# Attention stage of a fused kernel: PSUM banks split by use, the turning of outputs one step later, and row sums of squares taken after the biases

## The chip, the core and the metric

The kernel runs on one NeuronCore of one Trainium2 chip. The metric is the device time of one execution in microseconds (us). Five engines run their own instruction streams in order and wait for each other through semaphores: TensorE (PE), VectorE (DVE), ScalarE (ACT), GpSimd (POOL) and SyncE (SP, which here issues all transfers).

## The reference

```
def phi(x):
    proj = np.einsum('bhsd,md->bhsm', x, omega)
    sq = np.sum(x * x, axis=-1, keepdims=True) / 2.0
    h = proj - sq
    h = h - np.max(h, axis=-1, keepdims=True)
    return np.exp(h) / np.sqrt(m)
q_p, k_p = (phi(q_s), phi(k_s))
kv = np.einsum('bhsm,bhsd->bhmd', k_p, v)
z = np.sum(k_p, axis=2)
num = np.einsum('bhsm,bhmd->bhsd', q_p, kv)
den = np.einsum('bhsm,bhm->bhs', q_p, z)[..., None] + 1e-06
return (num / den).astype(np.float32)
```

This linear attention (batch 4, 8 heads, 576 positions, 64 wide, 128 features, all fp32) is followed by two feed-forward stages on the 2304 tokens: one gated by SiLU, and one of 8 experts that are all computed and mixed by weights. Those two are most of the time and are not touched by the change.

## The kernel before

**Stages.** The attention comes first and is a software pipeline written by hand. Its inputs are cut into 36 chunks of 128 partitions x 512 elements (8 groups of 64). Chunk 0 and chunk 17 are k tails (the last 64 positions of all heads), 18 and 35 are q tails; of the others the odd ones are k and the even ones q. A step of the pipeline does one piece of work for each of several chunks: `ORDER` (line 64) is a list of pairs of a piece and its lag, and in step s a piece with lag n is done for chunk s - n. The list is walked once per step, and each engine executes its instructions in the order in which the walk emits them. So `ORDER` sets the order on every engine.

**The pieces**, by line:
- `s0` (L481 to L484, POOL): squares a chunk of the next step and adds them pairwise, 64 to 16. `s0r` (L491, L492, DVE) adds up the rest and puts the sum of squares into `tri`.
- `s2p` (L510, PE): 16 matmuls project a chunk into two PSUM banks. `s2m` (L514, DVE, twice) takes the maxima from the banks; `s2b` and `s2c` (L518, L522, DVE) make the bias `bi` of them and of the sum of squares; `s2x` (L529, ACT, 8 instructions) takes the exponentials from the two banks.
- `s3`: for k, 40 matmuls with v (L550, PE) into a bank `kv`; for q, 8 transposes (L554, PE) into two banks. `s3a` (ACT) copies them to SBUF: L563 for k, L567 twice for q.
- `s4` (L580, PE): 32 matmuls of a q chunk with `kv` into two banks; `s4d`, `s4r`, `s4n` (L592, L597, L602, DVE) divide by the denominator.
- `s5` (L612, PE): 4 transposes turn the output of a q chunk into one bank; `s5a` (L623, ACT) copies it to `xh`, `s5b` (L628, DVE) writes the rest, bank less `xh`, to `xl`.
- `pump`: two slots in a step, each of which does one item of background work, the conversion of the next stage's weights. A task of 10 items has DVE items L198, L200, L202, L205, L207, ACT items L196 and L180 (the latter in the slot of L202), and POOL items L211, L214, L182; the other slots are empty. Six tasks are queued for the attention, from step 3 on.

In an even step PE thus projects a k chunk and does L580 and L554 for q chunks; in an odd step it projects a q chunk and does L550 for a k chunk. A pair of steps handles one k and one q chunk.

**Banks.** The eight PSUM banks are handed out in rings (`RINGS`): each use takes the next bank of its ring, and uses whose rings are equal share one turn.

**Buffers.** `xx`, the squares, lies in the fourth quarter of the tile `at0`, and the chunks themselves turn in the other three.

**End.** From step NCH + 1 = 37 on, each step also calls `next(m1)`, which emits 12 matmuls of the first feed-forward stage (L700 to L702), and the rings change to `DRAIN`.

Of the kernel before, what the change touches and what calls it, by code (L numbers as in the profile page):

```python
# [11 lines left out]
F32 = mybir.dt.float32  # L12
F32R = mybir.dt.float32r
# [7 lines left out]
P = 128  # L21
B, H, S, D = 4, 8, 576, 64
# [29 lines left out]
class Kernel:  # L52
    def __init__(self, tc, x, v, vt, omega, wg, wv, wo, w2g, w1, w2, out):
# [7 lines left out]

    ORDER = [("s3a0", 3), ("s0r", 0), ("s5a", 7), ("s2p", 1), ("s2m0", 1), ("s40", 4), ("s41", 4),
# [3 lines left out]
    RINGS = dict(tr3=(0, 3), tr5=(4, 5, 6, 7, 2, 1), pr=(4, 5, 6, 7, 2, 1), nu=(4, 5, 6,  # L68
                 7, 2, 1), a=(0, 1, 2, 3), b=(4, 5, 6, 7))

    DRAIN = dict(RINGS, tr3=(4, 5), tr5=(4, 5), nu=(6, 7))


    EARLY = 1
# [287 lines left out]
    def run(self):  # L362
        tc, nc = self.tc, self.nc
        with ExitStack() as ctx:
            self.cst = ctx.enter_context(tc.tile_pool(name="cst", bufs=1))
            self.raw = ctx.enter_context(tc.tile_pool(name="raw", bufs=1))
            self.ar1 = self.cst.tile([P, 6144], F32R, name="ar1")
            self.ar2 = self.cst.tile([P, 4096], F32R, name="ar2")
            self.af = ctx.enter_context(tc.tile_pool(name="af", bufs=1))
            psum = ctx.enter_context(tc.tile_pool(name="psum", bufs=1, space=PSUM))  # L370
            self.banks = [psum.tile([P, 512], F32, tag=f"b{i}", name=f"bank{i}") for i in range(4)]
            upper = ExitStack()
            psum = upper.enter_context(tc.tile_pool(name="upper", bufs=1, space=PSUM))
            self.banks += [psum.tile([P, 512], F32, tag=f"b{i}", name=f"bank{i}") for i in range(4, 8)]
            self.turns, self.rings, self.nquad = {}, self.RINGS, 0
            ident = self.cst.tile([P, P], F32, name="ident")
            make_identity(nc, ident)
            self.ident = ident
            self.xh = self.cst.tile([P, KC, NTOK], F32R, name="xh")
            self.xl = self.cst.tile([P, KC, NTOK], F32R, name="xl")  # L380
            self.cv = self.af.tile([P, 1024], I32, tag="cv", name="cv")
            park = ctx.enter_context(tc.tile_pool(name="park", bufs=1, space=bass.MemoryType.DRAM))
            self.park = park.tile([P, NB, KC, NBK], F32, name="parked")
            self.w1f = park.tile([P, NG2, 14, 512], F32, name="w1forms")
            self.w2f = park.tile([P, NG2, 7, 2, 2, 256], F32, name="w2forms")
            self.pd = park.tile([(NT - 6) * E, P], F32, name="pweights")
            with tc.manual_schedule():
                m1 = self.moe1()
                self.attention(m1)
                for _ in m1:  # L390
                    pass
                rest = self.moe2()
                upper.close()
                psum = ctx.enter_context(tc.tile_pool(name="pairs", bufs=1, space=PSUM))
                self.pairs = [psum.tile([P, 1024], F32, tag=f"b{i}", name=f"pair{i}") for i in range(2)]
                self.thirds(*rest)
# [3 lines left out]
    def attention(self, m1):  # L400
        tc, nc = self.tc, self.nc
        if True:
            af, ident = self.af, self.ident
            t0 = af.tile([P, 4, 512], F32, tag="t0", name="at0")
# [10 lines left out]
            def turn(name, n):  # L415
                rot[name] = (rot.get(name, -1) + 1) % n
                return rot[name]
# [8 lines left out]
            w = 8 * ZW  # L426
            vzts = [t4[:, NVZ + i] for i in range(2)] + [bx[:, 2048 + i * w:2048 + (i + 1) * w].rearrange(
                "p (a d) -> p a d", d=ZW) for i in range(2)]
            xts = [bx[:, i * 512:(i + 1) * 512] for i in range(4)]

            chunks = [("k", 0, None, None)]
# [8 lines left out]
            NCH = len(chunks)  # L440
# [5 lines left out]
            def load(i):  # L446
                side, bp, hp, j = chunks[i]
                c = st[i]
                n = 8 if hp is None else 2 * hp + j
                k = turn("x", 3)  # L450
                xt = xts[turn("xt", 4)]
                c["xt"] = xt.rearrange("p (a t) -> p a t", t=P)
                c["x"] = t0[:, k].rearrange("p (a d) -> p a d", d=D)
                for w, t in ((1, xt), (0, t0[:, k])):
                    nc.sync.dma_start(t, self.x["qk".index(side), w, bp, n])
                c["idx"] = (lambda a, h: 2 * a + h) if hp is None else (lambda a, h: 4 * h + a)

            def loadv(i):
                side, bp, hp, j = chunks[i]
                c = st[i]  # L460
                if side == "q":
                    return
                if hp is None:
                    c["vz"] = vzts[2 * bp:2 * bp + 2]
                    for j in range(2):
                        nc.sync.dma_start(c["vz"][j].rearrange("p a d -> p (a d)"), self.vt[bp, j])
                else:
                    z = c["vz"] = vz[nvz[0] % NVZ]
                    nvz[0] += 1
                    nc.sync.dma_start(z.rearrange("p a d -> p (a d)"), self.v[bp, 2 * hp + j])  # L470

            def s0(i):
                c = st[i]
                sqv = c["x"]
                if i < self.EARLY:
                    c["xx"] = t2[:, i].rearrange("p (a d) -> p a d", d=D)
                    c["tri"] = sm.tile([P, 8, 3], F32, tag="tri", name=f"tri{i}", bufs=4)
                    nc.scalar.activation(c["xx"], sqv, AF.Square)
                    return
                xx = t0[:, 3].rearrange("p (a d) -> p a d", d=D)  # L480
                nc.gpsimd.tensor_tensor(xx, sqv, sqv, op=ALU.mult)  # L481
                c["tri"] = sm.tile([P, 8, 3], F32, tag="tri", name=f"tri{i}", bufs=4)
                nc.gpsimd.tensor_tensor(xx[:, :, 0:32], xx[:, :, 0:32], xx[:, :, 32:64], op=ALU.add)
                nc.gpsimd.tensor_tensor(xx[:, :, 0:16], xx[:, :, 0:16], xx[:, :, 16:32], op=ALU.add)  # L484
                c["xx"] = xx
# [144 lines left out]

            pump = lambda i: self.attn_pump()
            fns = dict(s0=s0, s0r=s0r, s2=s2, s2p=s2p, s2b=s2b, s2c=s2c, s4r=s4r, s5=s5, s5a=s5a, s5b=s5b, pump=pump)
            halves = dict(s2m=s2m, s2x=s2x, s3=s3, s3a=s3a, s4=s4, s4d=s4d, s4n=s4n)

            def stage(n):
                if n in fns:
                    return fns[n]
                g, h = halves[n[:-1]], int(n[-1])
                return lambda i: g(i, h)

            order = [(stage(n), k) for n, k in self.ORDER]
            nc.sync.dma_start(om, self.omega)
            nc.vector.tensor_scalar(om, om, SCALE, None, op0=ALU.mult)
            load(0)
            load(1)
            s0(0)
            for step in range(NCH + 7):
                if step == NCH + 1:
                    self.rings = self.DRAIN
                if step + 2 < NCH:  # L650
                    load(step + 2)
                if step == 0:
                    loadv(0)
                if step + 1 < NCH:
                    loadv(step + 1)
                for fn, n in order:
                    i = step - n
                    if 0 <= i < NCH:
                        fn(i)
                self.attn_hook(step)  # L660
                if step >= NCH + 1:
                    next(m1)

    def attn_hook(self, step):
# [10 lines left out]
    def moe1(self):  # L675
# [43 lines left out]
        def ounit(g, b, us):  # L719
# [29 lines left out]
            if g == NG1 - 1 and b >= 2:  # L749
# [3 lines left out]
                else:  # L753
                    src = t4[:, 3:7, :] if b == 4 else tt[b][:, 0:4, :]
                    nc.sync.dma_start(self.park[:, b], src)

        self.side = self.sums()
        self.m1_open = True
        pend = None
# [779 lines left out]
```

## Time and profile before

| | us |
|---|---|
| median of 3 runs | 2054.8 (2054.72 to 2054.96) |
| profiled execution | 2054.87 |
| its span, first to last instruction | 2053.1 |
| PE busy in the span | 2016.2 (98%) |
| DVE, ACT, POOL busy | 1363.7, 805.5, 1035.1 |
| attention: first of 12 matmuls of the next stage starts at | 141.31 |
| exponentials of chunk 0, 9, 35 start at | 11.10, 41.36, 138.61 |

The span is 1.77 us shorter than the profiled execution. The attention takes the first 7% of it. A row of the timeline merges instructions of one line that follow each other on an engine; "x8" is their count, and in brackets stand the idle time of the engine before them and what ended it.

### The profile page before, as it was taken

The page shows a single profiled execution, that of the slowest core. Times are in us where ns is not written, and L with a number is a line of the kernel's source. Part 1 is how long each engine was busy: PE and PEld are TensorE (multiplying, and loading weights), DVE is VectorE, ACT ScalarE, POOL GpSimd, SP SyncE. Part 2 cuts the span into 40 slices and gives each one's busy share as a digit, 9 for nine tenths or more (in the row PEclk, how much of TensorE's full clock was granted, in tenths as well). Part 3 has the DMA queues.
Part 4 walks back from the last instruction along what each step waited for, and adds up shares of the span by engine and source line. Part 5 has one row for each costly group of instructions (what it writes and reads, how often), then busy time and mean ns, then how long its engine had stood idle before and what let it go on. Part 6 is the DMA issues. An engine that isn't in the chain of part 4 may idle for free.

```text
span 2053.1 us, 34001 instructions
## 1 busy us (share of the span) xinstructions
PE 2016.2 (98%) x12556; PEld 1948.0 (95%) x12556; DVE 1363.7 (66%) x2320; ACT 805.5 (39%) x1805; POOL 1035.1 (50%) x1019
## 2 busy tenths in 40 slices
PE   7899999999999999999999999999999999999998
PEld 6789999999998899899898999999999999999998
DVE  6876788778657654454455666666778766666666
ACT  7874433333345344344343433333233433232322
POOL 6755666656425455554752443434454544444443
PEclk9999999999999999999999999999999999999999
DMA  7635555556226657667668888888878887788784
GB/s 245 218 120 164 162 188 182 178 164 190 76 99 241 241 203 275 233 242 281 226 248 295 259 264 260 258 263 286 272 248 277 289 258 261 263 257 261 246 267 153
DMA packets 238133, 467.84 MB, mean 228 GB/s; under 512 B 20272, under 2 KB 110096, under 8 KB 233872
## 3 DMA queue, kind: packets, MB, share of 16 engines
q1 hardware_dynamic: 237968, 465.68, 68.1%
q8 instruction: 99, 1.62, 0.3%
q14 instruction: 66, 0.54, 0.1%
HBM read 340.25 MB, written 125.35 MB: 227 GB/s over the span
## 4 chain that ended last, share of the span: by engine, by line
PE 91%; DVE 5%; POOL 2%; issue 1%; ACT 1%; DMA 0%; SPq 0%; DVEq 0%; POOLq 0%; ACTq 0%
PE bank L1061 12%; PE bank L1309 7%; PE bank L1311 7%; PE bank L1310 7%; PE pair L1401 7%; PE pair L1403 7%; PE pair L1402 7%; PE bank L700 5%; PE bank L701 5%; PE bank L702 5%; PE bank L1002 4%; PE bank L1004 4%; PE bank L1003 4%; PE bank L732 2%; PE bank L733 2%; PE bank L734 2%
## 5 line engine op out<-in xcount | busy, mean ns | idle before, releaser
L1413 DVE TENSOR_TENSOR sums<-pair,sums 128x768 f32<-128x768 f32 x209 | 198.6, 951 | 43.6 <-PE pair L1403 43.6
L1309 PE MATMUL bank<-xh,ar 128*128 128x384 f32 x564 | 188.5, 334 | 0.9 <-DVE last L1347 0.9
L1311 PE MATMUL bank<-xh,ar 128*128 128x384 f32 x564 | 188.4, 334 | 0.0
L1310 PE MATMUL bank<-xl,ar 128*128 128x384 f32 x564 | 188.4, 334 | 0.0
L1077 DVE SCALAR_TENSOR_TENSOR ac<-bank,mt,ac 128x512 f32<-128x512 f32 x84 | 63.1, 751 | 130.7 <-PE bank L1061 130.7
L1401 PE MATMUL pair<-xh,ar 128*128 128x384 f32 x344 | 115.0, 334 | 0.2 <-DVE sums L1413 0.2
L1403 PE MATMUL pair<-xh,ar 128*128 128x384 f32 x344 | 114.9, 334 | 0.0
L1402 PE MATMUL pair<-xl,ar 128*128 128x384 f32 x344 | 114.9, 334 | 0.0
L1309 PEld LDWEIGHTS bank<-xh,ar 128*128 128x128 f32 x564 | 105.9, 188 | 1.3 <-DVE last L1347 1.2
L1311 PEld LDWEIGHTS bank<-xh,ar 128*128 128x128 f32 x564 | 105.9, 188 | 0.0
L1310 PEld LDWEIGHTS bank<-xl,ar 128*128 128x128 f32 x564 | 105.9, 188 | 0.0
L714 ACT CAST ar<-mt 128x384 fp32r<-128x384 f32 x72 | 37.0, 514 | 169.0 <-DVE mt L711 169.0
L700 PE MATMUL bank<-xh,ar 128*128 128x384 f32 x288 | 96.7, 336 | 0.1
L702 PE MATMUL bank<-xh,ar 128*128 128x384 f32 x288 | 96.2, 334 | 0.0
L702 PE MATMUL bank<-xh,ar1b 128*128 128x384 f32 x288 | 96.2, 334 | 0.0
L701 PE MATMUL bank<-xl,ar 128*128 128x384 f32 x288 | 96.2, 334 | 0.0
L700 PE MATMUL bank<-xh,ar1b 128*128 128x384 f32 x288 | 96.2, 334 | 0.0
L701 PE MATMUL bank<-xl,ar1b 128*128 128x384 f32 x288 | 96.2, 334 | 0.0
L1002 PE MATMUL bank<-xh,ar 128*128 128x384 f32 x264 | 89.2, 338 | 0.9 <-DVE mt L1036 0.6
L1004 PE MATMUL bank<-xh,ar 128*128 128x384 f32 x264 | 88.6, 336 | 0.1
L529 ACT ACTIVATE at<-bank,bi 128x128 f32<-128x128 f32 x288 | 78.4, 383 | 26.0 <-DVE bi L522 18.8
L1003 PE MATMUL bank<-xl,ar 128*128 128x384 f32 x264 | 88.3, 335 | 0.0
(370 smaller groups left out, 6637.6 us busy)
## 6 DMA issues: line engine op xcount, KB each, us to landing
ar<-w2forms SPq DMA_DIRECT2D x144, 512.0 KB, 4.4
ar<-w1forms SPq DMA_DIRECT2D x141, 512.0 KB, 4.8
ar1b<-w1forms SPq DMA_DIRECT2D x62, 512.0 KB, 4.8
ar1b<-w2forms SPq DMA_DIRECT2D x61, 512.0 KB, 4.4
w2forms<-ar SPq DMA_DIRECT2D x224, 128.0 KB, 4.0
w1forms<-ar SPq DMA_DIRECT2D x22, 1280.0 KB, 6.9
sumsraw<-in_w_dram SPq DMA_DIRECT2D x32, 512.0 KB, 4.4
w2forms<-sumsraw SPq DMA_DIRECT2D x128, 128.0 KB, 2.7
```

What stands on the lines that cost most here:

```text
L700: nc.tensor.matmul(t, hi[:, c, fs], self.xh[:, c, cs], start=(c == 0), stop=False)
L701: nc.tensor.matmul(t, hi[:, c, fs], self.xl[:, c, cs], start=False, stop=False)
L702: nc.tensor.matmul(t, lo[:, c, fs], self.xh[:, c, cs], start=False, stop=(c == KC - 1))
L1002: nc.tensor.matmul(g, ah[:, c, :], bh[:, c, :], start=(first and c == 0), stop=False, skip_group_check=not first)
L1061: nc.tensor.matmul(y, a, w[:, fi % 2, ds], start=(first and x == 0 and k == 0 and fi == fis[0]), stop=(last and x == 1 and fi == fis[-1]))
L1309: nc.tensor.matmul(g, w[:, 0, d], bh[:, d, :], start=bool(first and d == 0), stop=False, skip_group_check=not first)
L1310: nc.tensor.matmul(g, w[:, 0, d], bl[:, d, :], start=False, stop=False, skip_group_check=not first)
L1311: nc.tensor.matmul(g, w[:, 1, d], bh[:, d, :], start=False, stop=(d == 1), skip_group_check=not first)
L1401: nc.tensor.matmul(y, w[:, k, 0, ds], h, start=(k == 0), stop=False)
L1402: nc.tensor.matmul(y, w[:, k, 0, ds], l, start=False, stop=False)
L1403: nc.tensor.matmul(y, w[:, k, 1, ds], h, start=False, stop=(k == 1))
L1413: v.tensor_tensor(a[n], pair, a[n], op=ALU.add)
```

## The change

It rewrites `ORDER` and `RINGS`, gives the squares two buffers of their own, and starts the next stage's matmuls one step later.

- **Banks**: projections turn in banks 4 to 7, L554 and L612 share banks 0 and 3, `kv` and L580 share banks 2 and 1. Before, projections, L612, `kv` and L580 shared one ring of six (4, 5, 6, 7, 2, 1), and L554 had 0 and 3 alone.
- **Order**: `s5` moves from lag 6, at the end of a step, to lag 7, before `s3` of the same step, with `s5a` and `s5b` behind it; `s5a` comes after both `s3a`, where it stood between them. `s0r` moves from ahead of the maxima to behind `s2c` and `s5b`.
- **Buffers**: the squares take turns in two buffers in the place of the later tile `ar2`, which is therefore made when the next stage begins; the chunks turn in all four quarters of `at0`.

```
-    ORDER = [("s3a0", 3), ("s0r", 0), ("s5a", 7), ("s2p", 1), ("s2m0", 1), ("s40", 4), ("s41", 4),
-             ("s2m1", 1), ("s2b", 1), ("s2c", 1), ("s3a1", 3), ("s0", -1), ("pump", 2), ("s2", 0),
-             ("s30", 2), ("s2x0", 1), ("s31", 2), ("s4d0", 4), ("s5", 6), ("s5b",
-             7), ("s2x1", 1), ("s4d1", 4), ("pump", 3), ("s4r", 4), ("s4n0", 4), ("s4n1", 4)]
...
+    ORDER = [("s3a0", 3), ("s2p", 1), ("s2m0", 1), ("s3a1", 3), ("s40", 4), ("s41", 4), ("s5", 7), ("s5a", 7),
+             ("s2m1", 1), ("s2b", 1), ("s2c", 1), ("s5b", 7), ("s0r", 0), ("s0", -1), ("pump", 2), ("s2", 0),
+             ("s30", 2), ("s2x0", 1), ("s31", 2), ("s4d0", 4), ("s2x1", 1), ("s4d1", 4), ("pump", 3),
+             ("s4r", 4), ("s4n0", 4), ("s4n1", 4)]
+    RINGS = dict(tr3=(0, 3), tr5=(0, 3), pr=(4, 5, 6, 7), nu=(2, 1), a=(0, 1, 2, 3), b=(4, 5, 6, 7))
+
+    DRAIN = dict(RINGS, tr3=(4, 5, 6, 7), tr5=(4, 5, 6, 7), nu=(4, 5, 6, 7))
...
+            sq = self.cst.tile([P, 4096], F32, tag="ar2", name="squares")
+            sqs = [sq[:, i * 512:(i + 1) * 512] for i in range(2)]
...
-                k = turn("x", 3)
+                k = turn("x", 4)
...
-                xx = t0[:, 3].rearrange("p (a d) -> p a d", d=D)
+                xx = sqs[turn("xx", 2)].rearrange("p (a d) -> p a d", d=D)
...
-                if step >= NCH + 1:
+                if step >= NCH + 2:
                     next(m1)
```

**On PE**, from the end of an even step through an odd step to the start of the next even one, before (the number behind "bank" is the bank; "waits" names the engines whose semaphores the row waits for):

```order
L612 MATMUL bank5_77<-ident_80,at3_99 128x128 x4
L510 MATMUL bank6_78<-at6_102,turned_104 128x128 [waits DMAHW6_49,Activation_49]
L510 MATMUL bank7_79<-at6_102,turned_104 128x128 [waits DVE_49,Activation_49]
...
L550 MATMUL bank2_71<-at4_100,at1_97 64x66 [waits DMAHW0_49,DVE_49,Activation_49]
...
L510 MATMUL bank1_70<-at6_102,turned_104 128x128 [waits DMAHW1_49,DVE_49]
L510 MATMUL bank4_76<-at6_102,turned_104 128x128 [waits DVE_49]
```

and now, from L580 of the even step on:

```order
L580 MATMUL bank1_69<-at5_100,at2_97 64x66 [waits DVE_49]
...
L580 MATMUL bank2_70<-at5_100,at2_97 64x66 [waits Activation_49]
...
L554 MATMUL bank0_68<-ident_79,at1_96 128x128 x4
L554 MATMUL bank3_71<-ident_79,at1_96 128x128 [waits DVE_49]
...
L510 MATMUL bank4_75<-at6_101,turned_103 128x128 [waits DMAHW6_49]
...
L612 MATMUL bank0_68<-ident_79,at3_98 128x128 [waits Activation_49]
...
L550 MATMUL bank1_69<-at4_99,at1_96 64x66 [waits DMAHW0_49,DVE_49]
...
L510 MATMUL bank6_77<-at6_101,turned_103 128x128 [waits DMAHW1_49]
```

The projections (L510) wait for their input alone. L612 stands between the q projection and L550, writes the bank that L554 has just filled, and waits for ACT; so does the second half of L580.

**On ACT** in the same odd step, now, behind the exponentials of the k chunk (banks 6 and 7):

```order
L529 ACTIVATE at1_96<-bank7_78,bi19_1163 128x128 [waits Activation_49] x3
L567 COPY at2_97<-bank0_68 128x512 [waits PE_49]
L567 COPY at2_97<-bank3_71 128x512 [waits PE_49]
L623 CAST xh_84<-bank0_68 128x512 [waits PE_49]
L529 ACTIVATE at1_96<-bank4_75,bi20_1212 128x128 [waits DVE_49,Activation_49]
```

The bank that L612 writes and L623 reads, bank 0 here, is the one that the first L567 of the same step has to empty first.

**On DVE** in an odd step, now, between the bias of the q chunk and the maxima of the next k chunk (`bank6`; L204 and L206 are the lines L205 and L207 of before):

```order
L522 TENSOR_REDUCE bi14_860<-tri14_785 128x8 [waits DVE_49]
L628 TENSOR_TENSOR xl_85<-bank3_71,xh_84 128x512 [waits Activation_49]
L491 TENSOR_REDUCE at6_101<-squares_104 128x8 [waits Pool_49]
L492 TENSOR_REDUCE tri15_856<-at6_101 128x8 [waits DVE_49]
L204 SCALAR_TENSOR_TENSOR cv_86<-m1raw0_1_0_486,cv_86 128x512
L206 TENSOR_SCALAR m1raw0_1_0_486<-cv_86 128x512 [waits DVE_49]
L514 TENSOR_REDUCE tri15_856<-bank6_77 128x4 [waits PE_49]
```

Before, the same instructions stood between this bias and that L514, but with the first background item ahead of L628, the second ahead of L491, and with the sum of squares of the chunk after; now L628 and the sum come first, and both background items stand right before L514.

## Rows read from the trace of the kernel before

**Rows 1.** Busy time of each engine in stretches of 20 us, with counts.

```profile
80.00:100.00 20.00, 17.52 (x316) 15.36 (x318) 17.54 (x53) 17.38 (x58) 15.12 (x19) 1.00 0.61 199
140.00:160.00 20.00, 19.85 (x166) 18.54 (x166) 11.66 (x25) 10.93 (x23) 6.36 (x7) 1.00 0.01 2
```

**Rows 2.** Waits from 20 to 140 us: total, times, longest.

```profile
POOL at L481 <- DVE at L491: 17.4, 17, 2.3
PE bank L510 <- ACT at L529: 8.8, 14, 1.1
```

**Rows 3.** Timeline: exponentials of chunks 0, 9 and 35.

```profile
11.10 2.18 ACT L529 ACTIVATE at<-bank,bi 128x128 f32<-128x128 f32 x8 [5.41 <-DVE bi L522]
...
41.36 2.17 ACT L529 ACTIVATE at<-bank,bi 128x128 f32<-128x128 f32 x8 [0.65 <-DVE bi L522]
...
138.61 2.18 ACT L529 ACTIVATE at<-bank,bi 128x128 f32<-128x128 f32 x8 [0.20 <-DVE den L592]
```

**Rows 4.** Timeline of one pair of steps.

```profile
83.91 1.35 PE L580 MATMUL bank<-at,at 128*64 128x66 f32 x32
...
85.19 1.10 PE L554 MATMUL bank<-ident,at 128*128 128x128 f32 x8
85.39 0.33 ACT L563 ACTIVATE at<-bank 128x132 f32<-128x132 f32 x1
...
86.12 0.60 PE L612 MATMUL bank<-ident,at 128*128 128x128 f32 x4
86.15 2.18 ACT L529 ACTIVATE at<-bank,bi 128x128 f32<-128x128 f32 x8 [0.43 <-DVE den L592]
...
88.17 0.64 ACT L567 COPY at<-bank 128x512 f32<-128x512 f32 x1
...
88.43 0.69 PE L550 MATMUL bank<-at,at 128*64 128x66 f32 x16
88.50 0.28 DVE L491 TENSOR_REDUCE at<-at 128x8 f32<-128x128 f32 x1 [1.30 <-POOL at L484]
88.63 0.66 ACT L623 CAST xh<-bank 128x512 fp32r<-128x512 f32 x1
...
88.91 1.28 DVE L514 TENSOR_REDUCE tri<-bank 128x4 f32<-128x512 f32 x2
...
89.75 1.16 PE L510 MATMUL bank<-at,turned 64*128 64x128 f32 x16
...
90.51 0.68 DVE L628 TENSOR_TENSOR xl<-bank,xh 128x512 fp32r<-128x512 f32 x1
90.71 2.18 ACT L529 ACTIVATE at<-bank,bi 128x128 f32<-128x128 f32 x8 [0.37 <-DVE bi L522]
...
91.11 0.69 DVE L198 TENSOR_SCALAR cv<-m1raw 128x512 int32<-128x512 int32 x1
```

**Rows 5.** The chain that ended last: start, us, what.

```profile
131.31 0.45 PE bank L612 x4
```

**Rows 6.** Background items, 20 to 140 us: duration in ns, least/median/most.

```profile
L198 DVE TENSOR_SCALAR cv<-m1raw x5: 417/418/694, 33.7 to 109.3; 128x512 int32<-128x512 int32 x5
...
L200 DVE TENSOR_SCALAR cv<-cv x6: 418/570/683, 21.2 to 113.2; 128x512 f32<-128x512 f32 x6
...
L202 DVE TENSOR_SCALAR cv<-cv x6: 409/420/539, 21.7 to 114.4; 128x512 int32<-128x512 int32 x6
...
L205 DVE SCALAR_TENSOR_TENSOR cv<-m1raw,cv x6: 681/714/930, 24.3 to 116.7; 128x512 int32<-128x512 int32 x6
...
L207 DVE TENSOR_SCALAR m1raw<-cv x6: 419/532/571, 25.0 to 117.5; 128x512 int32<-128x512 int32 x6
...
L180 ACT CAST ar<-cv x5: 667/667/669, 39.9 to 115.4; 128x512 fp32r<-128x512 f32 x5
```

**Rows 7.** Timeline of DVE at the start.

```profile
6.44 0.17 DVE L492 TENSOR_REDUCE tri<-at 128x8 f32<-128x16 f32 x1
8.90 0.29 DVE L491 TENSOR_REDUCE at<-at 128x8 f32<-128x128 f32 x1 [2.28 <-POOL at L484]
```

More of the change, by code (lines that the diff above doesn't have):

```diff
@@ L59, in __init__ @@
         self.bg = deque()
-    ORDER = [("s3a0", 3), ("s0r", 0), ("s5a", 7), ("s2p", 1), ("s2m0", 1), ("s40", 4), ("s41", 4),
[3 rows of a table removed]
-    RINGS = dict(tr3=(0, 3), tr5=(4, 5, 6, 7, 2, 1), pr=(4, 5, 6, 7, 2, 1), nu=(4, 5, 6,
-                 7, 2, 1), a=(0, 1, 2, 3), b=(4, 5, 6, 7))
-    DRAIN = dict(RINGS, tr3=(4, 5), tr5=(4, 5), nu=(6, 7))
+    ORDER = [("s3a0", 3), ("s2p", 1), ("s2m0", 1), ("s3a1", 3), ("s40", 4), ("s41", 4), ("s5", 7), ("s5a", 7),
[4 more added lines that the diff above has]
+    DRAIN = dict(RINGS, tr3=(4, 5, 6, 7), tr5=(4, 5, 6, 7), nu=(4, 5, 6, 7))
     EARLY = 1
@@ L367, in run @@
             self.ar1 = self.cst.tile([P, 6144], F32R, name="ar1")
-            self.ar2 = self.cst.tile([P, 4096], F32R, name="ar2")
             self.af = ctx.enter_context(tc.tile_pool(name="af", bufs=1))
@@ L755, in ounit @@
                     nc.sync.dma_start(self.park[:, b], src)
+        self.ar2 = self.cst.tile([P, 4096], F32R, tag="ar2", name="ar2")
         self.side = self.sums()
```

## Prediction, made before the changed kernel ran

> **What bounds the kernel now.** I first read the busy time by stretches. From 140 us on PE is busy 19.85 of 20 us; before, in the attention, no engine is full: between 80 and 100 us PE has 17.52, DVE 17.54 and ACT 17.38 of 20 [rows 1]. The 1900 us after the attention are PE's own work, which the change does not alter, so only the first 140 us can give or take time, and a shift of the moment at which PE is full shifts the end by as much. Next I read the waits of that stretch: POOL waits 17.4 us for L491 to free the one buffer of squares, and PE waits 8.8 us at L510 for exponentials to free a bank [rows 2]; DVE in turn waits for POOL, as the 1.30 us ahead of one L491 show [rows 4]. So three engines wait in a ring, and the change cuts two links of it: a second buffer of squares, and banks of the projections' own. Last, the pace: the exponentials of chunk 9 start at 41.36 and those of chunk 35 at 138.61 [rows 3], 97.25 us for 13 pairs of steps, 7.48 us a pair. DVE's own work in a pair is 17.54/20 of that, 6.56 us. This would be the pace if nothing but DVE bounded.
>
> **The change part by part.** *Squares and sums.* With two buffers POOL may run most of a step ahead. Its 15.12 of 20 us [rows 1] are 5.7 us a pair, so it drops out. *Banks of the projections.* A projection takes banks whose exponentials ended a step ago; the wait at L510 goes.
>
> *The shared banks of L554 and L612* are where I expect the time to go. In the order of PE, L612 now stands ahead of L550 in the odd step, and its bank is the one that the first L567 of that step empties. That L567 follows the exponentials of the k chunk on ACT. Queued on PE behind the waiting L612 are L550 and the next k projection, and for this projection wait the maxima, the bias, and the next exponentials of a k chunk. That closes a loop of one pair, and each of its links has a row:
>
> - exponentials, first to the start of L567: 88.17 - 86.15 = 2.02; L567 itself 0.64 [rows 4]
> - ACT to PE: the exponentials end at 86.15 + 2.18 = 88.33, L550 starts at 88.43 [rows 4]: 0.10
> - L612 x4 up to what follows: 0.45 [rows 5]
> - L550, 40 matmuls, from 88.43 to the next L510 at 89.75: 1.32; L510 1.16 [rows 4]
> - PE to DVE: I take 0.05, since the first maximum needs its bank alone, which is full just before the last matmul (bounds 0 and the 0.10 from ACT to PE)
> - maxima and bias, from the first L514 at 88.91 to the exponentials at 90.71, which waited for the bias: 1.80 [rows 4]
>
> 2.02 + 0.64 + 0.10 + 0.45 + 1.32 + 1.16 + 0.05 + 1.80 = 7.54 us. No pair with L612 and L550 can be faster, whatever the other engines do. There are 12 such pairs between chunks 9 and 35; in the one with the k tail there is no L550, which leaves 6.2, so DVE's work bounds it: 6.6. Together 12 x 7.54 + 6.6 = 97.1 against 97.25: **-0.2 us**. What the two cut links give, the shared bank takes back.
>
> *kv and L580 in two banks.* The second half of L580 now waits until L563 has emptied a bank of `kv`; L563 stands on ACT behind the exponentials of the q chunk, and L554 and the next q projection are queued behind on PE. This loop has 2.02 + L563 0.33 + 0.10 + half of L580 (85.19 - 83.91)/2 = 0.64 + L554 1.10 + L510 1.16 + 0.05 + 1.80 = 7.20 [rows 4]: shorter than the other, so hidden behind it.
>
> *Background items.* They now stand on DVE right behind the sum of squares, ahead of the maxima. Counted from the start of the k exponentials, the maxima of the next k chunk can start at 7.54 - 1.80 = 5.74. L612 starts at 2.02 + 0.64 + 0.10 = 2.76 and its last transpose ends 0.60 later, at 3.36; L623 follows at 3.46 and takes 0.66 [rows 4]; DVE's L628 waits for that until 4.22, takes 91.11 - 90.51 = 0.60, and the sum takes 88.91 - 88.50 = 0.41 [rows 4]: 5.23. So 0.51 us is left for two background items, and what goes beyond adds to the loop. Ten steps hold two tasks; the order on DVE puts these items into the five odd steps: L198, then L205 with L207, then none, then L200 with L202, then none. With the middle durations [rows 6] the excess is 0 + (0.71 + 0.53 - 0.51) + (0.57 + 0.42 - 0.51) = 1.21 us; with the longest 0.18 + 0.99 + 0.71 = 1.88. Once in ten steps L180, 0.67 [rows 6], stands on ACT between the k exponentials and L567, fully on the loop. Items last from step 3 to step 32; from chunk 9's step 10 on that is 23 steps, 2.3 rounds: 2.3 x (1.21 + 0.67) = 4.3, with the longest 2.3 x 2.55 = 5.9. If an item overlaps its neighbours it costs less; below, nothing at all. I take **+4.2 us**, bounds 0 and 5.9.
>
> Which duration is right depends on POOL. L198 took 0.417 to 0.694 us, L205 0.681 to 0.930 [rows 6], though the shapes are the same. The Trainium skill (SBUF — State Buffer, Who interferes with whom) says that a DVE instruction with two inputs in SBUF, or one that uses both its ports, and a GpSimd instruction that reads SBUF shut each other out, which speaks against the change, since POOL no longer pauses for DVE. By that rule the term would be the 5.9 of the longest rows, and the sum 2059.4; by the middle rows it is 4.3, and the sum 2057.8.
>
> *The start.* Before, the maxima of chunk 0 stood behind L491 at 8.90, which waited for POOL; L492 of chunk 0 had ended at 6.61 [rows 7]. They now follow directly: chunk 0 gains up to 8.90 + 0.41 - 6.61 = 2.7. Later chunks keep less, as chunk 2's projection, with a ring of four banks, now waits for chunk 0's exponentials. Bounds 0 and 2.7; I take **-1.4 us**.
>
> *The end.* Before, PE was all but full from 140 us on, 1.4 us after the last exponentials began [rows 1, 3]. Now the next stage's matmuls come a step later, and the L580 of chunk 34 stands ahead of them and waits for the L567 behind those exponentials, 2.02 + 0.64 + 0.10 = 2.76 after they began. That is 2.76 - 1.4 = 1.4 us of PE, less the 8 transposes of chunk 35, 1.1 [rows 4], which wait for the same exponentials and fall into it: **+0.3 us**, bounds 0 and 1.4.
>
> *Costed at nothing:* the fourth quarter for chunks, the place of `ar2` (both only free buffers earlier or before anyone asks), and all transfers, whose order does not change.
>
> **The sum:** -0.2 + 4.2 - 1.4 + 0.3 = +2.9. On the profiled 2054.87 this gives 2057.8, and the median of the runs is 0.07 lower: **2057.7 us**, that is +0.14%. Changes under 0.2% (4.1 us) I count as no change; a measurement of this kernel can hardly tell them.
>
> **The rivals.**
> - *Each background item falls wholly on the loop* (slower). It decides if L628 starts 0.5 us later than I have it, because L623 waits behind the second L567 or the bias of the q chunk is late; then there is no slack. All five DVE items at their longest, 3.42, with L180 0.67 make 4.09 a round, 2.3 x 4.09 = 9.4: 2054.8 - 0.2 + 9.4 - 1.4 + 0.3 = 2062.9. For it speak the many in-order waits that meet there; against it that L628's work stays the same.
> - *Background items hide wholly.* Then the loop alone stands: 2054.8 - 0.2 - 1.4 + 0.3 = 2053.5. For it speaks that DVE has 7.54 - 6.56 = 1 us to spare in a pair; against it that the items come in lumps.
> - *DVE becomes the bound* (faster). If L612 does not hold up L550, because the copy comes in time, a pair takes 6.56: 13 x 0.92 = 12.0 us less, with start and end 2054.8 - 12.0 - 1.4 + 0.3 = 2041.7. The removed waits speak for it; against it each link of the loop, which only a row that I misread could break.
>
> **How the numbers follow.** The forecast, part of the items beside the loop, gets 0.52; items wholly on the loop 0.30; items hidden 0.12; DVE as the bound 0.06. From 2053 to 2063 lie the forecast, the hidden items and the slower rival up to its worked-out time; the tail above that and the fast case are left out, together not 2 in 10. Faster by over 0.2% is the last case alone, 0.06. No change takes the forecast's larger part (its own range is 2055 to 2060) and the hidden items, 0.60; slower takes the rest, 0.34.
>
> **What the profile would show.** If the steps are right: no wait of POOL at L481 for L491 and none of PE at L510 for ACT; in their place PE idle ahead of L612, ended by ACT's L567, about 1 us in a pair; ACT idle ahead of the k exponentials for the bias; DVE idle ahead of L628 for L623; 7.54 us from one k chunk's exponentials to the next where there are no items, and half a microsecond to one more where there are. The exponentials of chunk 0 would start near 8.4. The prediction is wrong if L612 finds its bank free, or if the pairs without items take other than 7.5 us.

## The result, and the profile after

The changed kernel takes **2070.89 us** (median of 6 runs, 2065.51 to 2073.28) against 2054.76 us for the kernel before beside it: a ratio of 1.0077, 95% interval 1.0066 to 1.0087. It is slower by 0.8%; the prediction was 2057.7 us, at most 2063. The profiled execution took 2070.31 us, 15.44 more than that of before.

The milestones of [rows 3], in the timeline of the changed kernel (ACT, chunks 0, 9 and 35; then PE, the first matmul of the next stage):

```profile
8.40 2.17 ACT L529 ACTIVATE at<-bank,bi 128x128 f32<-128x128 f32 x8 [2.62 <-DVE bi L522]
...
42.33 2.17 ACT L529 ACTIVATE at<-bank,bi 128x128 f32<-128x128 f32 x8 [1.83 <-PE bank L554]
...
152.75 2.17 ACT L529 ACTIVATE at<-bank,bi 128x128 f32<-128x128 f32 x8 [1.39 <-DVE den L592]
...
157.76 0.44 PE L700 MATMUL bank<-xh,ar 128*128 128x384 f32 x1
```

Chunk 0 is 2.70 us early, chunk 9 already 0.97 late. Between chunks 9 and 35 lie 110.42 us in place of 97.25: **13.17 of the 15.44 us are lost there.** From chunk 35 to L700 it is 5.01 in place of 2.70; what follows L700 took 1911.76 us before and 1910.59 now, which gives 1.17 back.

The windows that answer to [rows 1] (PE, PEld, DVE, ACT, POOL busy with counts, granted clock, DMA share, GB/s):

```profile
80.00:100.00 20.00, 14.85 (x254) 12.93 (x250) 17.42 (x45) 14.68 (x49) 14.01 (x17) 0.91 0.54 178
...
140.00:160.00 20.00, 17.59 (x274) 14.80 (x272) 12.95 (x40) 14.14 (x45) 3.70 (x6) 1.00 0.23 80
```

PE, ACT and POOL do less in the same 20 us; DVE is as busy as before, yet finishes 45 instructions in place of 53. Its instructions have become longer. The waits from 20 to 150 us, for [rows 2] (total, times, longest):

```profile
POOL squares L481 <- DVE at L491: 30.3, 22, 3.1
...
ACT at L529 <- DVE bi L522: 23.0, 19, 2.6
PE bank L612 <- ACT at L567: 20.5, 12, 3.8
...
PE bank L580 <- ACT at L563: 8.9, 11, 1.9
ACT xh L623 <- PE bank L612: 4.5, 14, 0.7
...
DVE xl L628 <- ACT xh L623: 3.6, 4, 1.4
```

L510 no longer waits for ACT, and L612 waits for L567, as predicted. But POOL's wait at L481 for L491, predicted to go, grew from 17.4 to 30.3 us. What it does is in the timeline of an even step, DVE and POOL:

```profile
101.57 0.28 DVE L491 TENSOR_REDUCE at<-squares 128x8 f32<-128x128 f32 x1
...
101.88 0.17 DVE L492 TENSOR_REDUCE tri<-at 128x8 f32<-128x16 f32 x1
101.93 1.04 POOL L481 TENSOR_TENSOR squares<-at 128x512 f32<-128x512 f32 x1 [0.76 <-DVE at L491]
101.97 1.28 DVE L199 TENSOR_SCALAR cv<-cv 128x512 f32<-128x512 f32 x1
...
103.05 0.78 POOL L483 TENSOR_TENSOR squares<-squares 128x256 f32<-128x256 f32 x1
103.17 0.22 DVE L592 TENSOR_SCALAR den<-bank 128x4 f32<-128x4 f32 x2
103.31 0.80 DVE L201 TENSOR_SCALAR cv<-cv 128x512 int32<-128x512 int32 x1
```

L491 frees the buffer that L481 waits for, and L481 starts 0.04 us ahead of the background item. The item (L199 is L200 of before) then takes 1.28 us in place of 0.42. The second item, L201, starts while POOL does the next sum of the squares (L483) and takes 0.80 in place of 0.41. The durations of the items, from 20 to 150 us (ns, least/median/most), for [rows 6]:

```profile
L197 DVE TENSOR_SCALAR cv<-m1raw x5: 778/1144/1286, 33.9 to 121.1; 128x512 int32<-128x512 int32 x5
...
L199 DVE TENSOR_SCALAR cv<-cv x5: 1278/1280/1281, 38.5 to 125.8; 128x512 f32<-128x512 f32 x5
...
L201 DVE TENSOR_SCALAR cv<-cv x6: 799/832/836, 19.6 to 127.1; 128x512 int32<-128x512 int32 x6
...
L204 DVE SCALAR_TENSOR_TENSOR cv<-m1raw,cv x6: 683/1545/1548, 22.4 to 129.9; 128x512 int32<-128x512 int32 x6
...
L206 DVE TENSOR_SCALAR m1raw<-cv x6: 558/804/840, 23.1 to 131.5; 128x512 int32<-128x512 int32 x6
```

The medians sum to 5.6 us a task, against 2.65 before.

The pairs, each from the start of one k chunk's exponentials to the next one's, in us, worked out from the starts of L529 in the profiled executions (the last four columns are experiments below):

| pair ending at chunk | before | change | sum last | items ahead of sum | turn's own bank | own bank, sum last |
|---|---|---|---|---|---|---|
| 11 | 7.12 | 7.83 | 7.62 | 7.62 | 8.15 | 7.14 |
| 13 | 8.22 | 8.22 | 7.62 | 7.62 | 7.90 | 7.05 |
| 15 | 7.61 | 9.89 | 8.40 | 7.89 | 9.89 | 8.05 |
| 17 | 7.31 | 7.59 | 7.59 | 7.60 | 6.44 | 6.44 |
| 19 (k tail) | 7.60 | 8.88 | 7.62 | 7.62 | 8.79 | 7.60 |
| 21 | 6.93 | 9.02 | 7.62 | 9.15 | 9.50 | 6.76 |
| 23 | 8.21 | 8.02 | 7.62 | 7.62 | 7.66 | 7.42 |
| 25 | 7.60 | 9.90 | 8.40 | 7.89 | 9.90 | 8.04 |
| 27 | 7.36 | 9.14 | 7.62 | 7.62 | 6.47 | 6.46 |
| 29 | 7.58 | 8.88 | 7.62 | 7.62 | 8.77 | 7.59 |
| 31 | 6.94 | 7.83 | 7.62 | 7.62 | 8.15 | 7.14 |
| 33 | 8.16 | 7.61 | 7.62 | 7.62 | 7.10 | 7.05 |
| 35 | 6.61 | 7.61 | 7.62 | 7.62 | 7.02 | 7.02 |

The last two pairs have no items on VectorE: 7.61. The items repeat every five pairs, so the pairs that end at 21 and 27 should be those of 11 (or 31) and 17. They are longer by 9.02 - 7.83 = 1.19 and 9.14 - 7.59 = 1.55, and in both the granted clock had fallen. Windows ahead of the first and in it, then PE's timeline there:

```profile
84.40:87.10 2.70, 0.00 (x0) 0.00 (x0) 2.63 (x8) 2.36 (x9) 2.09 (x2) 1.00 0.74 241
87.10:90.50 3.40, 3.06 (x40) 2.73 (x42) 3.30 (x10) 1.92 (x6) 2.74 (x3) 0.51 0.12 45
```

```profile
87.44 1.12 PE L612 MATMUL bank<-ident,at 128*128 128x128 f32 x4 [3.84 <-ACT at L567]
88.49 1.15 PE L550 MATMUL bank<-at,at 128*64 128x66 f32 x16
```

PE did nothing for 3.84 us, of which the first window shows 2.70, and ran the next stretch at half clock, 1.2 GHz: its four transposes took 1.12 us in place of 0.60, sixteen matmuls of L550 1.15 in place of 0.69 [rows 4]. The stretch from 114.4 us, behind a gap of 2.46 us ahead of L612, has the same clock (0.51). The Trainium skill (TensorE: Matmul & The Clock Gate, HAM oscillation — how this bites in real kernels) says that gaps on TensorE bring it back to the lower clock; these two stretches agree, though not every gap of this length was followed by one (see the part on half clock below).

So the 13.17 us are: the plain pair, 13 x 7.61 = 98.93 for 97.25, +1.7; the half clock, 1.19 + 1.55 = 2.7; and what is left above 7.61 in pairs with items, 110.42 - 98.93 - 2.7 = 8.8.

### The profile page after: what moved, and what is told of

Its sections match the earlier page's. It is cut to its first block, busy times and chain, and to the rows that moved or that the text cites. A ratio compares the mean times of both kernels' runs of the same rounds, so it can differ in the third digit from the quotient of the medians.

```text
span 2068.4 us, 33928 instructions
## 1 busy us (share of the span) xinstructions
PE 2017.7 (98%) x12556; PEld 1947.7 (94%) x12556; DVE 1376.5 (67%) x2320; ACT 805.8 (39%) x1805; POOL 1036.2 (50%) x1019
## 4 chain that ended last, share of the span: by engine, by line
PE 91%; DVE 5%; ACT 2%; DMA 1%; issue 0%; SPq 0%; DVEq 0%; ACTq 0%
PE bank L1062 12%; PE bank L1310 7%; PE bank L1311 7%; PE bank L1312 7%; PE pair L1402 7%; PE pair L1403 7%; PE pair L1404 7%; PE bank L700 5%; PE bank L701 5%; PE bank L702 5%; PE bank L1003 4%; PE bank L1005 4%; PE bank L1004 4%; PE bank L732 2%; PE bank L733 2%; PE bank L734 2%
## 5 line engine op out<-in xcount | busy, mean ns | idle before, releaser
L700 PE MATMUL bank<-xh,ar 128*128 128x384 f32 x288 | 96.6, 335 | 0.0
L700 PE MATMUL bank<-xh,ar1b 128*128 128x384 f32 x288 | 96.2, 334 | 0.0
L529 ACT ACTIVATE at<-bank,bi 128x128 f32<-128x128 f32 x288 | 78.2, 385 | 32.7 <-DVE bi L522 26.2
```

Source lines behind the costliest of these rows:

```text
L700: nc.tensor.matmul(t, hi[:, c, fs], self.xh[:, c, cs], start=(c == 0), stop=False)
```

## The experiments

**Two theories**, whose costs can add. *A*: because the sum of squares (L491) stands right ahead of an item, it frees POOL's L481 at the moment at which the item starts; the two shut each other out, the item grows by the time of L481, and the maxima behind it are late. *L*: what costs is the bank that L554 and L612 share, with its loop of 7.54 us a pair. A third, *end*: what costs is that the next stage's matmuls come a step later. The kernel before measured 2054.4 to 2054.8 us beside all of them.

### Theory A

**Sum of squares last in the step**, so that it is followed by the maxima, which read PSUM, and no longer by an item:

```
-             ("s2m1", 1), ("s2b", 1), ("s2c", 1), ("s5b", 7), ("s0r", 0), ("s0", -1), ("pump", 2), ("s2", 0),
+             ("s2m1", 1), ("s2b", 1), ("s2c", 1), ("s5b", 7), ("s0", -1), ("pump", 2), ("s2", 0),
...
-             ("s4r", 4), ("s4n0", 4), ("s4n1", 4)]
+             ("s4r", 4), ("s4n0", 4), ("s4n1", 4), ("s0r", 0)]
```

> The changed kernel with the sum of squares (L491, L492) moved to the very end of a step, so that maxima, which read PSUM, follow it on DVE and no background item. Theory A (the item and POOL's L481 start at the same moment, because L491 releases both, and the item then waits until L481 is through): the items fall from 1.14 to 1.55 us back to 0.4 to 0.9, pairs of steps with items from 8.8 to about 8.0 us, the total to 2060 to 2065. Rival B (the items are long because POOL is busier wherever they stand): they stay above 1 us, the total stays at 2068 to 2073.

Measured: 2059.64 us, ratio 1.0024 (1.0015 to 1.0033), 11.3 less than the change and a little below what A expected. The items, from 20 to 140 us:

```profile
L199 DVE TENSOR_SCALAR cv<-cv x5: 415/419/561, 35.9 to 113.6; 128x512 f32<-128x512 f32 x5
...
L204 DVE SCALAR_TENSOR_TENSOR cv<-m1raw,cv x6: 681/748/1094, 21.1 to 116.4; 128x512 int32<-128x512 int32 x6
```

They are short again, no stretch of the attention is at half clock in the profiled execution (at 2057.13 us the fastest of the 11), and the pairs are 7.62 almost everywhere (table): on this loop short items cost nothing. POOL still waits 19.1 us at L481 for L491; so it is not the wait that costs, but what stands on DVE when it ends. The two pairs of 8.40 hold L179 (L180 of before), 0.67 us on ACT between the k exponentials and L567, as the prediction had it. L612 still waits 16.1 us for L567. What is left above the kernel before is theory L's, as the run with both edits shows below.

**Eight buffers for squares in place of two**, the order left alone; POOL then no longer waits for L491:

```
-            sqs = [sq[:, i * 512:(i + 1) * 512] for i in range(2)]
+            sqs = [sq[:, i * 512:(i + 1) * 512] for i in range(8)]
...
-                xx = sqs[turn("xx", 2)].rearrange("p (a d) -> p a d", d=D)
+                xx = sqs[turn("xx", 8)].rearrange("p (a d) -> p a d", d=D)
```

> The changed kernel with eight buffers of squares in place of two, so that L491 releases nothing on POOL soon. Theory A: POOL's wait for L491 (30.3 us) goes, the items meet L481 only by chance and take 0.5 to 1.0 us on average, the total falls to 2062 to 2068. Rival B: POOL is no less busy, the items stay above 1 us, 2068 to 2073.

Measured: 2062.33 us, ratio 1.0038 (1.0024 to 1.0052). L481 now waits for its input only:

```profile
POOL squares L481 <- DMA at<-in_x_dram: 13.6, 10, 4.5
```

The medians of L199 and L204 fall to 0.45 and 0.81 us in the whole attention, L201's stays at 0.84, and some items still meet a square by chance (L199 up to 1.22). So it is the meeting, not the order by itself, that makes an item long.

**Items ahead of the sum of squares**; everything on PE and the place of the sum behind the bias stay (on POOL the items go ahead of the squares too, and on ACT both of a step ahead of its exponentials, so that L179 leaves the loop):

```
-             ("s2m1", 1), ("s2b", 1), ("s2c", 1), ("s5b", 7), ("s0r", 0), ("s0", -1), ("pump", 2), ("s2", 0),
-             ("s30", 2), ("s2x0", 1), ("s31", 2), ("s4d0", 4), ("s2x1", 1), ("s4d1", 4), ("pump", 3),
+             ("s2m1", 1), ("s2b", 1), ("s2c", 1), ("s5b", 7), ("pump", 2), ("pump", 3), ("s0r", 0), ("s0", -1), ("s2", 0),
+             ("s30", 2), ("s2x0", 1), ("s31", 2), ("s4d0", 4), ("s2x1", 1), ("s4d1", 4),
```

> The changed kernel with both slots of background items moved ahead of the sum of squares (L491) of the same step; the sum keeps its place behind the bias, PE's order and the banks stay those of the change. Theory A (an item is long because L491 frees POOL's L481 just before it, and the two shut each other out): POOL is now waiting while the items run, so their medians fall back to 0.42 to 0.75 us (L200-like 1.28 to 0.42, L204 1.55 to 0.7), the waits of PE at half clock in the attention go, and the time is 2058 to 2064. Rival B (what costs is that an item stands in DVE's order ahead of the maxima, however long it takes by itself, so any place in the step costs the same): 2067 to 2073, with exponentials of chunk 9 to 35 more than 107 us apart.

Measured: 2059.26 us, ratio 1.002 (1.0011 to 1.0029). Rival B falls. In its timeline of an odd step on DVE, the same items in the same gap, but now ahead of L491, take 0.68 and 0.43:

```profile
98.62 0.69 DVE L628 TENSOR_TENSOR xl<-bank,xh 128x512 fp32r<-128x512 f32 x1
99.23 0.68 DVE L204 SCALAR_TENSOR_TENSOR cv<-m1raw,cv 128x512 int32<-128x512 int32 x1
99.95 0.43 DVE L206 TENSOR_SCALAR m1raw<-cv 128x512 int32<-128x512 int32 x1
100.29 0.28 DVE L491 TENSOR_REDUCE at<-squares 128x8 f32<-128x128 f32 x1
```

Of A's expectation one part missed: one stretch at half clock is left, from 80.8 us, after a gap of PE of 2.28 us ahead of L612. Its pair takes 9.15, the one five pairs earlier and later 7.62: 1.5 us again.

### Theory L

**Outputs turned into the ring of `kv`**, so that L612 and L554 no longer share a bank:

```
-    RINGS = dict(tr3=(0, 3), tr5=(0, 3), pr=(4, 5, 6, 7), nu=(2, 1), a=(0, 1, 2, 3), b=(4, 5, 6, 7))
+    RINGS = dict(tr3=(0, 3), tr5=(2, 1), pr=(4, 5, 6, 7), nu=(2, 1), a=(0, 1, 2, 3), b=(4, 5, 6, 7))
```

> The changed kernel with L612 in the ring of kv and L580 (banks 2 and 1) in place of that of L554 (0 and 3): its bank is then free since the division of the even step. Theory L (the bank shared with L567's copy makes the loop of 7.6 us): PE's wait at L612 for L567 (20.5 us) goes, pairs without items fall from 7.6 to at most 7.3, the next bound being L580 behind L563, worked out at 7.2. Items still stand behind L491, so they stay at 1.1 to 1.55 us (theory A). Total 2062 to 2068. Rival (the long items alone set the pace): 2068 to 2073 and pairs without items at 7.6.

Measured: 2063.06 us, ratio 1.0042 (1.0029 to 1.0054), 7.8 less than the change. The waits from 20 to 140 us:

```profile
PE bank L612 <- DVE at L602: 13.1, 7, 4.3
PE bank L580 <- ACT at L563: 11.8, 13, 1.4
```

L612 no longer waits for L567. The last two pairs, without items on VectorE, take 7.10 and 7.02 (those of 6.44 and 6.47, which have none either, follow the two longest): the loop through the shared bank was the limit, and the next one, L580 behind L563, holds from there on. The items are as long as in the change (L199 1.28, L204 1.55), and so are the pairs with items.

**L550 ahead of L612 on PE**, another way to take L612's wait off the projections:

```
-    ORDER = [("s3a0", 3), ("s2p", 1), ("s2m0", 1), ("s3a1", 3), ("s40", 4), ("s41", 4), ("s5", 7), ("s5a", 7),
+    ORDER = [("s3a0", 3), ("s2p", 1), ("s2m0", 1), ("s3a1", 3), ("s40", 4), ("s41", 4), ("s30", 2), ("s31", 2), ("s5", 7), ("s5a", 7),
...
-             ("s30", 2), ("s2x0", 1), ("s31", 2), ("s4d0", 4), ("s2x1", 1), ("s4d1", 4), ("pump", 3),
+             ("s2x0", 1), ("s4d0", 4), ("s2x1", 1), ("s4d1", 4), ("pump", 3),
```

> The changed kernel with the products of a step (L550, L554) ahead of the turning of outputs (L612) on PE; banks, DVE and ACT order unchanged. Theory L (L612 waits for the copy out of its bank and holds up L550 and the next projection): pairs without items fall from 7.6 to 6.6 to 6.9 us, the others by at least half a microsecond, the total to 2058 to 2064. Rival (the lengthened items alone set the pace, L612's wait is slack): pairs unchanged, 2068 to 2073.

Measured: 2074.78 us, ratio 1.01 (1.0086 to 1.0113): slower, and the expectation missed. Its waits:

```profile
ACT xh L623 <- PE bank L612: 17.1, 12, 3.6
PE bank L580 <- ACT at L563: 16.5, 12, 1.8
DVE xl L628 <- ACT xh L623: 12.5, 11, 2.3
```

The wait moved from PE to ACT. L623 stands in ACT's order ahead of the exponentials of the q chunk, and behind it DVE's L628 and the long items wait. The last two pairs take 7.24 and 7.63, not 6.6 to 6.9, and three stretches, from 44.3, 88.7 and 136.5 us, are at half clock. The run decides nothing about the loop; it shows that L612 has a second follower that can't wait either.

### Both, and the parts of the change by themselves

**Own bank and sum last** together (both edits above):

> As the run before, and the sum of squares at the end of a step as in e1. If the two theories add: items at 0.4 to 0.9 us, all pairs at 7.0 to 7.4 where e1 had 7.62, total 2052 to 2056. If the two costs are one and the same, as where the loop only hides the items: the total stays at e1's 2059.6, with pairs of 7.6.

Measured: **2051.70 us**, ratio 0.9986 (0.9977 to 0.9994), 19.2 less than the change where the two alone gave 11.3 and 7.8 (19.1): the costs add. It is 3.1 us (0.15%) below the kernel before; the interval leaves out 1, but it is less than the 0.2% that I count. The total lies just under the 2052 to 2056 expected; the pairs scatter more than expected, from 6.44 to 8.05, with a mean of 7.21. Its waits:

```profile
PE bank L580 <- ACT at L563: 12.7, 15, 1.3
ACT at L529 <- DVE bi L522: 7.9, 15, 0.7
```

**Own bank and items ahead of the sum** (both edits):

> The kernel with the turn's own bank (outputs turned into the ring of kv) and both item slots ahead of the sum of squares. If the two costs add, as in the kernel with the sum last, theory A gives short items and no loop at L612: 2050 to 2056. Rival B: as with the turn's own bank alone, 2061 to 2066.

Measured: 2052.28 us, ratio 0.9988 (0.9979 to 0.9997): the same again by the other order, as A expected.

**The kernel before with two buffers for squares and four quarters for chunks**, without the banks and the order of the change:

```
-                k = turn("x", 3)
+                k = turn("x", 4)
...
-                xx = t0[:, 3].rearrange("p (a d) -> p a d", d=D)
+                xx = sqs[turn("xx", 2)].rearrange("p (a d) -> p a d", d=D)
```

> The kernel before with two buffers of squares and four of chunks, and nothing else of the change. If the ring of waits between POOL and DVE was a cost by itself: POOL's wait for L491 falls well below 17.4 us, DVE's for POOL (8.2 us) goes, and the total falls by 2 to 8 us, to 2047 to 2053, as maxima and not items stand behind L491. If POOL, freed, runs into the items: they rise above 0.8 us and the total is 2055 or more.

Measured: 2054.38 us, ratio 0.9997 (0.9988 to 1.0006): no change, the expectation missed. Waits from 20 to 140 us (lines are one further on):

```profile
ACT at L530 <- DVE bi L523: 12.3, 17, 2.3
...
POOL squares L482 <- DMA at<-in_x_dram: 10.2, 7, 2.6
DVE tri L515 <- ACT at L530: 6.9, 9, 0.8
PE bank L511 <- ACT at L530: 6.9, 10, 1.5
```

POOL's 17.4 us for DVE are down to 1.8, and DVE's 8.2 us for POOL are gone, but the equal total hides a gain and a loss. Worked out as in the table, the pairs that end at 13, 17, 23, 27 and 33 take 7.28, 6.81, 7.19, 6.82 and 6.66 us in place of 8.22, 7.31, 8.21, 7.36 and 8.16. Those at 15 and 25, with four items each on VectorE, take 9.07 and 9.34 in place of 7.61 and 7.60. Together it is 96.63 us from chunk 9 to 35, for 97.25. The items have become longer here too:

```profile
L200 DVE TENSOR_SCALAR cv<-cv x6: 416/823/1189, 20.6 to 113.5; 128x512 f32<-128x512 f32 x6
```

Its median was 0.57 before, and the five medians sum to 3.52 us in place of 2.65. So the ring's link through POOL did cost time in the kernel before, and cutting it alone gave that time to longer items: POOL, freed, ran into them, as the second half of the expectation has it, though the medians are 0.61 to 0.82 and the total is not above 2055. The two buffers and the fourth quarter were not tried apart.

**The old end** (the next stage's matmuls from step NCH + 1, and the old `DRAIN`), on the change and on the best kernel:

```
-    DRAIN = dict(RINGS, tr3=(4, 5, 6, 7), tr5=(4, 5, 6, 7), nu=(4, 5, 6, 7))
+    DRAIN = dict(RINGS, tr3=(4, 5), tr5=(4, 5), nu=(6, 7))
...
-                if step >= NCH + 2:
+                if step >= NCH + 1:
```

> The changed kernel with the end of the kernel before alone undone. If the later start of the next stage costs about 1 us: 2069 to 2070, a change within the spread of the changed kernel's own runs (2065 to 2073); if the end is a main cost: 2066 or less.

> As e6, with the end of the kernel before: the next stage's matmuls from step 37 and its rings for the end. In the changed kernel they began 5.0 us after the last exponentials, before 2.7, and did 1.2 us of L580 earlier for it. If the later start costs the difference, this run is 1.1 us or more below e6, at 2050 to 2055, under the kernel before. If the end is hidden: the same as e6 within 0.5.

Measured: 2073.62 us, ratio 1.0084 (1.007 to 1.0097), and 2053.69 us, 0.9992 (0.9984 to 1.0001). Neither is faster than with the new end, and both miss what was expected: the first is 2.7 us above the changed kernel (its runs, 2069.34 to 2076.33, overlap with that one's), the second 2.0 above the best one. The profiled execution of the second has two stretches at half clock (from 26.0 and 80.6 us), so these 2.0 us are not the price of the old end alone. On the best kernel L700 comes 4.81 us after chunk 35's exponentials in place of 5.02, and the stage behind it takes 1911.9 in place of 1910.84: what starts earlier is paid back. So these two edits are not what holds L700 back. What does is in both tails, of the changed kernel first, then of the one with the old end:

```profile
156.40 0.69 DVE L628 TENSOR_TENSOR xl<-bank,xh 128x512 fp32r<-128x512 f32 x1 [2.61 <-ACT xh L623]
...
157.15 0.69 PE L580 MATMUL bank<-at,at 128*64 128x66 f32 x16 [1.01 <-DVE xl L628]
```

```profile
159.68 0.69 DVE L628 TENSOR_TENSOR xl<-bank,xh 128x512 fp32r<-128x512 f32 x1 [2.61 <-ACT xh L623]
...
160.43 0.66 PE L554 MATMUL bank<-ident,at 128*128 128x128 f32 x4 [2.88 <-DVE xl L628]
```

The last matmuls ahead of L700 wait for L628, which reads its bank, and L628 waits for L623 on ACT, behind the last exponentials. In the kernel before L628 came 3.17 us after these exponentials began, for 3.65 in the change, but L700 did not wait for it and started 0.47 us earlier.

## Why the prediction was wrong

**The step that failed is the term of the background items, +4.2 us with bounds 0 and 5.9.** It measured 8.8 us, and 2.7 more for half clock. Two things in it were wrong.

- Its durations came from the rows of before [rows 6], 2.65 us a task in the middle. The prediction's own order of DVE shows L491, L492 and an item in a row, and [rows 2] show that POOL waits for that L491: put together, L481 and the item start at the same moment every time. The premise that hid it was "Its 15.12 of 20 us are 5.7 us a pair, so it drops out". POOL keeps on waiting for L491, because two buffers let it run ahead only until both are full. The longest rows of before, taken as the upper bound, were no bound: there an item had at most 0.41 us of a running operation of the squares to wait for, in the changed kernel up to 1.00.
- The sentence on the Trainium skill (SBUF — State Buffer, Who interferes with whom) named the right mechanism, that the two shut each other out. The runs bear it out, with L481 first by 0.04 us. I gave it only the longest rows of before as its price. The nearest row for a full shut-out stands in the changed kernel alone, but the length of L481, 1.04 us, bounds what an item can lose to it.

With the middle durations of the changed kernel, the prediction's own count of the excess gives 0.63 + 1.84 + 1.60 and 0.67 for L180, 4.74 us a round, and 2.3 x 4.74 = 10.9: the durations are enough for the whole miss. The count itself was on the safe side when the items are short: with items ahead of the sum two items of 0.68 and 0.43 cost 7.89 - 7.62 = 0.27, where the slack of 0.51 would have given 0.6. It left out the items of the even steps, which hold up the maxima and the bias of the q chunk: where L199 and L201, or L204 and L206, stand there, L628 starts 4.76 to 5.03 us after the k exponentials in place of 4.22 (five of the 13 pairs; 4.01 to 4.45 in the others). The pairs that end at 11 and 31, with no other items on VectorE, take 7.83 for 7.61.

**The loop** was right: 7.61 us in pairs without items for the 7.54 worked out, with L612 waiting for L567, and 7.02 to 7.14 once its bank is moved, against 7.20 for the loop through L580 and L563. The sum of it was off by 1.9 us (98.93 for 97.1), half of it the pair with the k tail, which I put at 6.6. With short items it took 7.62: there L628 waits for L623, and the two items, the sum and the maxima follow on DVE.

**Half clock** wasn't in the prediction. Between chunks 9 and 35 it came behind gaps ahead of L612 of 3.84 and 2.46 us. But another gap of 2.46 us in the same execution was not followed by it, nor one of 2.67 with the sum last, nor one of 3.39 with eight buffers; so the length of the gap alone does not decide it.

**The start**: chunk 0's exponentials at 8.40, as predicted, but nothing of it is left at chunk 9 (+0.97 for -1.4). With the sum last chunk 9 starts at 38.89, 2.47 early; in the change the long items of the first steps and a half-clock stretch from 25.7 us took that. The kernel before ran at half clock from 11.2 to 21.4 us, which the prediction left out; what that is worth was not taken apart.

**The end**: +2.31 to L700 less 1.17 given back, +1.1 for +0.3, inside its bounds. The first half of chunk 34's L580 starts at 155.45, 2.70 us after the exponentials, for the 2.76 worked out; the prediction lacks the second half's wait for L628.

Together 1.0 + 1.7 + 8.8 + 2.7 + 1.1, with 0.2 outside the span, is 15.5, the 15.44 us of the profiled executions but for rounding. Of the rivals, the slower one (items wholly on the loop, 2062.9) came nearest in number, but its price had the same wrong durations, and its condition, L628 half a microsecond late, held in five pairs of 13 only. That DVE becomes the bound did not come.

What stays open: why a low clock came behind some gaps and in some executions and not in others. The runs of the changed kernel spread over 7.8 us, those with the sum last over 4.2, those of the kernel before over 2.

## What to carry to other kernels

Where an instruction on VectorE frees a buffer that GpSimd waits for, look at what stands behind it on VectorE: an item like these here (TENSOR_SCALAR, SCALAR_TENSOR_TENSOR, from SBUF to SBUF) starts together with GpSimd and is held up; put one there that is not, here the maxima. A bank that two uses share ties their engines into a loop; add up its links before you give a use fewer banks, and find the next loop as well. A second buffer cuts a wait only if the engine behind it has the lead to fill it, and an engine that it frees works at other times than before: look at what it then meets.

## What was not expected of the hardware

- A meeting with L481 lengthens items of different kinds by the same amount: L199 from 0.418 to 1.280 us, L204 from 0.681 to 1.545, both by 0.86, with L481 itself at 1.04 and 1.00 of it still to run. In the twelve profiled executions 241 items of the attention started with more than 0.15 us of a GpSimd operation still to run; 238 of them were longer than the shortest of their kind by that rest less 0.12 to 0.14 us. In the other three both started within 0.01 us of each other, the item stayed short, and GpSimd's operation took 0.28 to 0.30 longer. So the later one waits and then runs; they don't share. The Trainium skill (SBUF — State Buffer, Who interferes with whom) states a full block until the first has finished; the traces agree, but for the 0.12 to 0.14 us.
- The reductions on VectorE were not held up: L491, from SBUF, took 0.27 to 0.29 us and each half of L514, from PSUM, 0.67 to 0.70, beside a GpSimd operation or not.
- A stretch at half clock cost 1.19, 1.55 and 1.53 us, read from pairs with the same work at either clock; two such pairs at full clock, those that end at 13 and 23, differ by 0.2.
